# A new order of all steps, with the identity compared on VectorE, its reversal copied from it and fewer index iotas

## The chip, the cores and the metric

The kernel runs on one NeuronCore of a Trainium2 chip. Its engines work side by side, each through its own instructions in order: TensorE (PE in the profile, with its weight loads as PEld), VectorE (DVE), ScalarE (ACT), GpSimd (POOL) and SyncE (SP), which here only issues DMAs. An engine waits for another one by semaphores. The metric is the device time of one execution in microseconds (us).

## The reference

Two layers in a row, in float32. First an attention with a feature map instead of a softmax, for 8 batches and 8 heads of 576 positions by 64:

```python
def phi(x):
    proj = np.einsum('bhsd,df->bhsf', x, w_phi)          # 64 -> 128 features
    proj = proj - np.max(np.abs(proj), axis=-1, keepdims=True)
    return np.concatenate([np.exp(proj), np.exp(-proj)], axis=-1)
q_p, k_p = phi(q), phi(k)
kv  = np.einsum('bhsf,bhsd->bhfd', k_p, v);   z = np.sum(k_p, axis=2)
num = np.einsum('bhsf,bhfd->bhsd', q_p, kv);  den = np.einsum('bhsf,bhf->bhs', q_p, z)
x = num / (den + 1e-6)                                   # heads side by side: (8, 576, 512)
```

Then a gated convolution over the sequence, done with Fourier transforms of length 576:

```python
x1, x2, x3 = np.split(x @ w_proj, 3, axis=-1)            # 512 -> 3 * 512
H = np.fft.rfft(filter_fft, n=S, axis=0)
x2_conv = np.fft.irfft(np.fft.rfft(x2, n=S, axis=1) * H, n=S, axis=1)
out = (x1 * x2_conv * x3) @ w_out
```

## The kernel before

The eight batches are called images here. For each image the kernel does the same chain of steps, and the steps of several images are interleaved. Nothing is scheduled at run time or by a planner inside the kernel: one string, `PLAN`, lists all steps in order, and `run` goes through it word by word and calls the method of that name. Each engine therefore executes its instructions in the order in which the words stand. A word reads `name,arguments@bank`: `ex,k,p,1,1@6` is the exponential, k side, positive sign, image 1, block 1, from PSUM bank 6; `ACT`, `DVE` or `POOL` among the arguments says which engine does the step.

PSUM has eight banks, and the plan says which a step uses. A step that writes a bank waits until the one before it there has been read, and readers of one bank on different engines follow each other in plan order.

**The start.** Nothing of the transforms comes from memory: cosine and sine tables are made on the chip. `gen_part` and `gen_rows` write indices with iotas on POOL (lines 344 to 361; the tiles `part`, `fr`, `nr`). `gen_cols` makes some forty column constants on DVE (lines 379 to 423). `gen_whole` rounds index times constant to a whole number on ACT (line 435), `gen_angles` subtracts it on DVE (line 452), and `gen_sin` takes the sine on ACT (line 467) into the tables `D`, `Dt` and `inv`. `gen_ident` and `gen_back` make an identity and a reversal matrix on POOL, each by an iota and a compare with a constant (lines 305 to 316). The identity serves PE's transposes (`pt`, `ptx`, `trm`), the reversal a product `D1m` that mirrors `D`, which `D1e` copies out with signs (line 333). `gen_neg` stores negated copies of two tables (line 996). `filt_load`, `filt_fold`, `H`, `H_ev` and `H_cp` transform the filter.

**One image.** `load` fetches q, k and v through POOL's DMA queue (line 586) with a cast to bfloat16. `trh` transposes q and k by DMA on SP's queue (line 598), for image 0 `pt` and `pte` do it on PE and an evacuating engine (lines 608, 288 and 290; 288 is an ACT copy, 290 a DVE copy). `Pk` and `Qn` are the projections, `maxk` and `maxq` the absolute maxima on DVE (line 703), `mhi`, `mlo`, `trm` and `trme` bring q's maxima into rows, `Pq` projects q again with the maxima subtracted on PE. `ex`, `exkt` and `exqt` are the exponentials on ACT (lines 689 to 697), `em` those of the maxima, `vs` scales v with them (line 750). `KV` sums keys by values on PE (line 765), `KVe` copies it out, `NE` and `NEt` make numerator and denominator (lines 779, 788), `rc`, `xn`, `rct` and `xnt` divide (lines 793 to 815). The sequence of 576 is cut as 9 times 64; the names that end in `t` handle the ninth part. `trx` and `trxt` transpose x by DMA on SP (lines 822, 827), for image 0 `ptx` and `ptxt` do it on PE (lines 832, 841).

`f1` and `f2` are two levels of folds, sums and differences (lines 852, 858; tiles `SD` and `xf`), `F` is the forward transform on PE (lines 864, 868), `Fe` and `Fet` copy it out, `X2` applies the second third of the weights in the transformed domain (line 886), `Y1` multiplies by the filter (line 896), `m3` adds pairs (line 900), `I` is the inverse transform (line 973), with `Ie`, `Ip` and `Im` as its evacuation and half sums (lines 977, 980). `X1` and `X3` are the other two projections (line 908; `X1a` and `X1b` are half of one each), `X1e` copies one out, `tm` multiplies by the other (line 961). `ym` multiplies both branches (line 1021), `O` is the last product (line 1032), `Oe` copies it out, `st` and `sh` store halves of it (line 1041): `st` on SP, `sh` on ACT's or SP's queue as the word says. The last image uses `J` and `yj` (lines 1011, 1015) instead of `I`, `Ip`, `Im` and `ym`.

**What orders POOL against DVE.** The method `port` adds a dependency: after certain steps on DVE (those in the tuple `PORT` with `DVE` in their word, `gen_angles` and `yt`) the next listed POOL step waits for the DVE instruction. So a POOL step of that kind can wait for work on DVE whose data it doesn't use.

## Time and profile before

| what | us |
|---|---|
| median of 3 runs | 304.31 |
| lowest and highest run | 304.29 and 306.02 |
| the profiled execution | 304.55 |
| its span, first to last instruction | 302.8 |

The profile is of one execution, so instruction times and waits come from a run that lies 0.24 us above the median; its span leaves out 1.75 us around the first and the last instruction. The engine table of the page gives each engine's busy time and its share of the span. The stretches give the same by stage, with the granted clock of TensorE and the share of the DMA engines. The chain of work that ended last goes back from the last instruction through what released each step. In a timeline row the numbers are start, duration, engine, line, operation and tiles, with the idle time ahead of it and what ended that in brackets. A row of a group has the count, then the busy time in us and the mean of one in ns.

### The profile page before, as it was taken

How to read it: one execution, taken by the hardware profiler on the slowest of the kernel's cores; microseconds unless marked ns; L12 is line 12 of the kernel's file. 1: busy time of each engine (PE TensorE's matmuls, PEld its weight loads, DVE VectorE, ACT ScalarE, POOL GpSimd, SP SyncE). 2: the span in 40 equal slices, each digit the busy share in tenths (PEclk: the TensorE clock that was granted, in tenths of full speed). 3: DMA queues.
4: the chain of work that ended last, by engine and by line, in shares of the span. 5: the costliest groups of instructions: out<-in, count | busy, mean ns of one | idle time of the engine just before them, and what ended most of it. 6: DMA issues, size and time to landing. Idle time of an engine off the chain costs nothing.

```text
span 302.8 us, 10174 instructions
## 1 busy us (share of the span) xinstructions
PE 269.7 (89%) x4253; PEld 198.2 (65%) x4289; DVE 258.9 (86%) x449; ACT 227.8 (75%) x407; POOL 219.7 (73%) x190
## 2 busy tenths in 40 slices
...
GB/s 135 214 203 133 187 142 154 205 117 132 146 191 157 125 106 181 164 170 135 184 214 130 97 115 166 127 189 83 131 40 59 110 69 2 36 98 87 2 157 192
DMA packets 71902, 39.98 MB, mean 132 GB/s; under 512 B 52208, under 2 KB 66672, under 8 KB 71856
## 3 DMA queue, kind: packets, MB, share of 16 engines
...
## 4 chain that ended last, share of the span: by engine, by line
PE 67%; DVE 13%; ACT 8%; issue 5%; POOL 4%; DMA 1%; SPq 0%; DVEq 0%; ACTq 0%
PE ps L908 17%; PE ps L886 9%; PE ps L1032 9%; PE ps L973 5%; PE ps L765 5%; PE ps L779 3%; DVE mq L703 3%; DVE mk L703 2%; PE ps L864 2%; PE ps L868 2%; PE ps L627 2%; PE ps L917 2%; PE ps L661 2%; PE ps L1011 2%; PE ps L667 1%
## 5 line engine op out<-in xcount | busy, mean ns | idle before, releaser
L908 PE MATMUL ps<-xT,wproj 128*128 128x256 bf16 x512 | 64.8, 273 | 0.2
L908 PEld LDWEIGHTS <-wproj 128*128 128x128 bf16 x512 | 47.7, 98 | 9.4 <-issue 0.4
L703 DVE TENSOR_REDUCE mk<-ps 128x8 f32<-128x1024 f32 (+1 forms) x40 | 43.8, 1109 | 4.5 <-PE ps L627 2.2
L703 DVE TENSOR_REDUCE mq<-ps 128x8 f32<-128x1024 f32 (+1 forms) x40 | 44.1, 1110 | 2.9 <-PE ps L642 1.5
L852 POOL TENSOR_TENSOR SD<-xn 128x512 bf16<-128x512 bf16 x29 | 33.1, 1153 | 15.6 <-ACT xn L805 4.0
L750 POOL TENSOR_TENSOR vm<-vn,vm 128x1152 bf16<-128x1152 bf16 x15 | 32.3, 2153 | 9.2 <-ACT Eqp L689 4.1
L750 POOL TENSOR_TENSOR vp<-vn,vp 128x1152 bf16<-128x1152 bf16 x15 | 32.3, 2153 | 5.7 <-ACT vp L744 5.6
L689 ACT ACTIVATE Eqp<-ps 128x1024 bf16<-128x1024 f32 x32 | 32.7, 1025 | 3.8 <-PE ps L667 3.1
L1021 POOL TENSOR_TENSOR yT<-cv,x1s 128x576 bf16<-128x576 f32 x23 | 29.2, 1280 | 8.6 <-DVE yT L1021 4.1
L689 ACT ACTIVATE Ekm<-ps 128x1024 bf16<-128x1024 f32 x32 | 32.7, 1038 | 3.2 <-PE ps L627 2.4
L689 ACT ACTIVATE Eqm<-ps 128x1024 bf16<-128x1024 f32 x32 | 32.8, 1024 | 2.9 <-PE ps L667 2.9
L1032 PE MATMUL ps<-wout,yT 128*128 128x512 bf16 x133 | 33.7, 379 | 0.8 <-issue 0.2
L858 POOL TENSOR_TENSOR xf<-SD 128x512 bf16<-128x512 bf16 x29 | 33.0, 1153 | 1.5 <-PE ps L627 0.7
L689 ACT ACTIVATE Ekp<-ps 128x1024 bf16<-128x1024 f32 x32 | 32.9, 1046 | 1.6 <-DVE mk L703 1.6
L900 POOL TENSOR_TENSOR T<-T,T 128x1024 bf16<-128x1024 bf16 x12 | 25.4, 2122 | 9.7 <-DVE T L896 6.7
L886 PE MATMUL ps<-wproj,XF 128*128 128x512 bf16 x111 | 30.5, 380 | 1.0 <-issue 0.2
L288 ACT CAST x1s<-ps 128x512 bf16<-128x512 f32 (+1 forms) x27 | 15.1, 562 | 19.4 <-PE ps L908 14.4
L980 DVE TENSOR_TENSOR cv<-es,ps 128x288 f32<-128x288 f32 x56 | 22.4, 447 | 2.7 <-ACT es L977 2.0
L973 PE MATMUL ps<-inv,T 128*128 128x288 bf16 x168 | 24.3, 286 | 0.2
L961 DVE TENSOR_TENSOR x1s<-ps,x1s 128x512 bf16<-128x512 f32 x32 | 21.6, 682 | 3.1 <-ACT x1s L288 1.6
L1032 PEld LDWEIGHTS <-yT 128*128 128x128 bf16 x144 | 13.3, 98 | 14.1 <-DVE yT L1015 0.5
L779 PE MATMUL ps<-KVs,Eqp 128*128 128x65 bf16 x256 | 19.5, 192 | 1.6 <-DVE x1s L965 0.9
...
## 6 DMA issues: line engine op xcount, KB each, us to landing
...
```

Source lines behind the costliest of these rows:

```text
L689: self.nc.scalar.activation(e, p, AF.Exp, bias=0.0, scale=1.0 if g == "p" else -1.0)
L703: self.nc.vector.tensor_reduce(out=out, in_=src, axis=AX.X, op=ALU.max, apply_absolute_value=True)
L750: self.eng(eng).tensor_tensor(out=t[:, :, :, 0:64], in0=self.at("vn", b)[:, 2 * X:2 * X + 2], in1=t[:, :, :, 64:65].to_broadcast([128, 2, ...
L779: self.mm(self.pb(u, 65 * a, 65 * a + 65), E, KVs[:, u, v, s, :], start=(s == 0), stop=(s == 1))
L852: self.eng(eng).tensor_tensor(out=o[:, :, 2 * i:2 * i + 2, :], in0=x[:, :, 0:2, :], in1=x[:, :, 2:4, :], op=ALU.subtract if i else ALU.add)
L858: self.eng(eng).tensor_tensor(out=o[:, :, 2 * i:2 * i + 2, :], in0=x[:, :, 0:4:2, :], in1=x[:, :, 1:4:2, :], op=ALU.subtract if i else ALU ...
L886: self.mm(self.pb(0), l, w[:, kt, 512:1024], start=(kt == 0), stop=(kt == 3))
L900: self.eng(eng).tensor_tensor(out=Y, in0=Y, in1=self.at(f"T{2 * e + 1}", b), op=ALU.add)
L908: self.mm(o[:, d], w[:, kt, f0 + 128 * m:f0 + 128 * m + 128], y[:, 1, ::-1, ::-1] if d else y[:, 0], start=(kt == 0 and not d), stop=(kt = ...
L973: self.mm(self.pb(e, 0, 288), l, inv[:, 2 * e + i if i < 2 else 4 + e, :], start=(i == 0), stop=(i == 2))
L1021: self.eng(eng).tensor_tensor(out=self.at("yT", b)[:, m, 0:SEQ], in0=self.at("cv", 4 * b + m).rearrange("p x h t -> p (x h t)"), in1=self. ...
L1032: self.mm(self.pb(0), y[:, kt, 128 * c:128 * c + 128], w[:, kt, :], start=(kt == 0), stop=(kt == 3))
```

## The change

Five things, all in the diff below.

- The identity's compare moves from POOL to DVE (`gen_ident,DVE`); its iota is a step of its own, `gen_idx`. `gen_ident` joins `PORT`, so the POOL step that follows it in the listed set waits for it.
- The reversal matrix is no longer made from a second iota and compare; `gen_back,ACT` copies the identity with its columns in reverse.
- The row indices come from five iotas instead of nine; the larger ones write both halves of a tile at once.
- `xnt`, the division of the ninth part, takes an engine; on ScalarE it is four multiplications. The new plan names DVE for all sixteen.
- All steps stand in a new order with other banks, and many change engine: `D1e` goes to ACT and `gen_whole,3` to DVE; of the folds `f1` and `f2`, six go from DVE to POOL and three the other way; of `m3`, two go to POOL and four to DVE; of `ym`, four go to POOL and one to DVE; evacuations change between ACT and DVE in both directions. `gen_neg` moves from the middle of image 0 to the sines. The stores of image 6 and the last image are split anew between ACT's and SP's queues.

The steps are the same in number and work on TensorE. Of the plan, the diff is cut to the start, a stretch of image 3 and the end.

```diff
 PORT = ("f1", "f2", "m3", "vs", "ym", "mlo", "filt_fold", "gen_ends", "gen_five",
-        "gen_whole", "H_cp")
+        "gen_whole", "gen_ident", "H_cp")
...
-w_load,phi gen_part gen_cols,0 loadh,q,0,0 filt_loadt loadh,q,0,1 filt_load,3 gen_rows,0 w_phi
-gen_cols,1 filt_load,2 gen_rows,1 gen_whole,ACT,2 gen_ident filt_load,0 gen_back gen_whole,ACT,3
-gen_one gen_whole,ACT,0 loadh,k,0,1 gen_angles,3 filt_load,1 load,q,1 gen_whole,ACT,4 pt,q,0,0,0@0
-gen_angles,0 pt,q,0,0,1@1 loadh,k,0,0 gen_angles,2 pte,ACT,q,0,0,0@0 w_load,proj,2 gen_angles,4
-pte,ACT,q,0,0,1@1 load,v,0 gen_sin,0 Qn,0,0@0 filt_fold,DVE,2 gen_sin,4 D1m@2 maxq,0,0@0
-filt_fold,POOL,0 pt,q,0,1,0@4 pt,q,0,1,1@5 zeros pt,k,0,1,0@0 pte,DVE,q,0,1,0@4 gen_sin,2
-pte,DVE,q,0,1,1@5 pt,k,0,1,1@1 D1e,DVE@2 filt_fold,POOL,1 Qn,0,3@4 pte,DVE,k,0,1,1@1 Qn,0,1@6
-pte,DVE,k,0,1,0@0 gen_sin,3 maxq,0,1@6 Pk,0,3@0 H,0@2 trh,q,1,1 Pk,0,2@6 H_ev,DVE,0@2 ex,k,p,0,3@0
...
-f1,DVE,0,1,0 ptx,0,3@3 mhi,1 rct,0@4 Pk,1,0@0 ex,k,m,1,1@6 f1,POOL,0,1,1 ptxe,DVE,0,1@2 xnt,0,1@4
-xnt,0,0@4 ptxe,ACT,0,3@3 maxk,1,1@6 load,v,1 ptxt,0@4 X1a,0,1@5 ex,k,p,1,0@0 w_load,proj,1 Pkt,1@2
...
-m3,DVE,2,1 KVe,ACT,3,1@4 Pkt,4@0 NE,3,1@2 ex,q,m,3,3@6 m3,DVE,2,0 X2,2,4@4 trh,q,5,0 rc,3,1@2
-maxkt,4@0 ex,q,p,3,3@6 X3,2,2@5 xn,DVE,3,1@2 exkt,p,4@0 trh,k,5,0 Y1,2,4@4 NE,3,3@6 exkt,m,4@0
-NE,3,2@2 f1,DVE,3,0,0 mhi,4 rc,3,3@6 NEt,3@0 mlo,POOL,4 xn,DVE,3,3@6 trh,k,5,1 f1,POOL,3,0,1 O,1,4@4
...
-Oe,ACT,6,2@7 O,7,2@6 yt,ACT,7 st,6,2 O,7,0@7 Oe,ACT,7,2@6 O,7,4@5 sh,SP,7,2,0 sh,ACT,7,2,1
-Oe,DVE,7,0@7 O,7,3@6 Oe,DVE,7,4@5 sh,SP,7,0,0 sh,ACT,7,0,1 O,7,1@7 Oe,DVE,7,3@6 sh,SP,7,4,0
-sh,ACT,7,4,1 Oe,DVE,7,1@7 sh,SP,7,3,0 sh,ACT,7,3,1 sh,SP,7,1,0 sh,ACT,7,1,1
+w_load,phi gen_part gen_idx gen_cols,0 loadh,q,0,0 filt_loadt loadh,q,0,1 zeros filt_load,2
+gen_ident,DVE gen_one gen_rows,0 gen_cols,1 filt_load,3 gen_rows,1 gen_whole,ACT,0 loadh,k,0,1
+gen_whole,ACT,2 filt_load,1 load,q,1 w_phi gen_angles,0 gen_whole,ACT,4 loadh,k,0,0 gen_angles,2
+filt_load,0 load,v,0 gen_sin,0 gen_whole,DVE,3 pt,q,0,0,0@0 w_load,proj,2 gen_back,ACT pt,q,0,0,1@1
+gen_angles,4 pte,ACT,q,0,0,0@0 pte,ACT,q,0,0,1@1 gen_sin,2 gen_angles,3 Qn,0,0@0 filt_fold,DVE,2
+pt,q,0,1,0@2 maxq,0,0@0 filt_fold,POOL,0 gen_sin,4 D1m@4 pt,q,0,1,1@3 pte,DVE,q,0,1,0@2 pt,k,0,1,0@0
+pte,DVE,q,0,1,1@3 pt,k,0,1,1@2 gen_neg pte,DVE,k,0,1,0@0 Qn,0,3@6 gen_sin,3 pte,DVE,k,0,1,1@2
+Pk,0,3@2 D1e,ACT@4 Qn,0,1@0 maxq,0,1@0 H,0@4 trh,q,1,1 H_ev,DVE,0@4 Pk,0,2@0 ex,k,p,0,3@2 maxq,0,3@6
...
+load,v,1 X1a,0,2@7 ex,k,m,1,0@4 X1b,0,2@7 maxkt,1@0 w_load,proj,1 X1a,0,3@2 X1e,ACT,0,1@6 maxk,1,0@4
+X3a,0,1@3 f2,POOL,0,1,0 exkt,m,1@0 ptxt,0@6 X1b,0,3@2 exkt,p,1@0 X1e,DVE,0,2@7 ptxte,ACT,0@6
...
+rc,3,0@4 xn,DVE,3,0@4 X2,2,1@6 ex,q,m,3,2@2 maxk,4,0@0 m3,POOL,2,1 KV,3,1@4 trxt,2 mhi,4
+X1e,ACT,2,2@7 Y1,2,1@6 Pkt,4@0 trx,3,0 Pq,3,3@2 exkt,m,4@0 X3,2,2@7 KVe,DVE,3,1@4 m3,POOL,2,0
...
+ex,q,p,3,3@2 st,0,2 NE,3,2@0 Y1,2,4@6 f1,POOL,3,0,1 NEt,3@4 rc,3,2@0 trh,k,5,0 NE,3,3@2 xn,DVE,3,2@0
+O,1,4@6 f1,POOL,3,0,0 rc,3,3@2 xn,DVE,3,3@2 X1t,2@0 rct,3@4 Oe,ACT,1,4@6 f2,POOL,3,0,0 trx,3,3
...
+Oe,DVE,7,3@2 sh,ACT,7,1,0 O,7,4@4 Oe,DVE,7,2@1 sh,SP,7,3,1 sh,ACT,7,3,0 sh,ACT,7,2,0 Oe,DVE,7,4@4
+sh,SP,7,2,1 sh,ACT,7,4,1 sh,ACT,7,4,0
...
-    def gen_ident(self):
-        g, s = self.nc.gpsimd, self.scr
-        kw = dict(allow_small_or_imprecise_dtypes=True)
-        idx = s.tile([128, 128], FP32, name="idx")
-        g.iota(idx, pattern=[[1, 128]], base=0, channel_multiplier=-1, **kw)
-        self.idx = idx
-        g.tensor_scalar(out=self.at("ident"), in0=idx, scalar1=0.0, scalar2=None,
-                        op0=ALU.is_equal)
-
-    def gen_back(self):
-        g, s = self.nc.gpsimd, self.scr
-        idx = s.tile([128, 128], FP32, name="idy")
-        self.back = s.tile([128, 128], BF16, name="back")
-        g.iota(idx, pattern=[[1, 128]], base=0, channel_multiplier=1,
-               allow_small_or_imprecise_dtypes=True)
-        g.tensor_scalar(out=self.back, in0=idx, scalar1=127.0, scalar2=None, op0=ALU.is_equal)
+    def gen_idx(self):
+        self.idx = self.scr.tile([128, 128], FP32, name="idx")
+        self.nc.gpsimd.iota(self.idx, pattern=[[1, 128]], base=0, channel_multiplier=-1,
+                            allow_small_or_imprecise_dtypes=True)
+
+    def gen_ident(self, eng):
+        self.eng(eng).tensor_scalar(out=self.at("ident"), in0=self.idx, scalar1=0.0, scalar2=None,
+                                    op0=ALU.is_equal)
+
+    def gen_back(self, eng):
+        self.back = self.scr.tile([128, 128], BF16, name="back")
+        self.copy(eng, self.back, self.at("ident")[:, ::-1])
...
-            g.iota(self.nr[:, 0:128], pattern=[[1, 4], [9, 32]], base=1, **kw)
-            g.iota(self.nr[:, 128:256], pattern=[[1, 4], [9, 32]], base=6, **kw)
+            g.iota(self.nr[:, 0:256], pattern=[[5, 2], [1, 4], [9, 32]], base=1, **kw)
...
-        for odd in range(2):
-            g.iota(self.fr[:, odd, 0], pattern=[[2, 144]], base=odd, **kw)
-            g.iota(self.fr[:, odd, 1, 0:16], pattern=[[2, 16]], base=256 + odd, **kw)
-            g.iota(self.fr[:, odd, 1, 16:144], pattern=[[2, 128]], base=odd, **kw)
+        g.iota(self.fr[:, :, 0], pattern=[[1, 2], [2, 144]], base=0, **kw)
+        g.iota(self.fr[:, :, 1, 0:16], pattern=[[1, 2], [2, 16]], base=256, **kw)
+        g.iota(self.fr[:, :, 1, 16:144], pattern=[[1, 2], [2, 128]], base=0, **kw)
...
+        for X in range(2):
+            for u in range(2):
+                self.nc.scalar.mul(o[:, X, u, :], n[r, X, u, w, 0:64], rt[r, 2 * X + u, w, :])
...
-        elif f in PORT and "POOL" in args or f in ("gen_ident", "gen_back", "gen_part", "gen_rows"):
+        elif f in PORT and "POOL" in args or f in ("gen_idx", "gen_part", "gen_rows"):
```

309 lines of the change are left out of this document (157 added, 152 removed).

## The prediction

> **What bounds the kernel now.** I read the page first, then busy time by stretches, then the chain that ended last.
>
> ```profile
> span 302.8 us, 10174 instructions
> ...
> PE 269.7 (89%) x4253; PEld 198.2 (65%) x4289; DVE 258.9 (86%) x449; ACT 227.8 (75%) x407; POOL 219.7 (73%) x190
> ...
> PE 67%; DVE 13%; ACT 8%; issue 5%; POOL 4%; DMA 1%; SPq 0%; DVEq 0%; ACTq 0%
> ```
>
> PE is busy 89% of the span and holds 67% of the chain. But an average hides the stages, so here are three stretches (PE, PEld, DVE, ACT, POOL busy, then the granted clock):
>
> ```profile
> 10.00:20.00 10.00, 6.68 (x74) 4.87 (x76) 8.55 (x19) 9.95 (x17) 6.18 (x3) 1.00 1.20 210
> ...
> 200.00:240.00 40.00, 39.54 (x606) 29.42 (x607) 34.72 (x58) 32.90 (x56) 34.08 (x26) 1.00 0.46 88
> ...
> 285.00:302.80 17.80, 12.19 (x77) 7.25 (x75) 8.80 (x13) 1.50 (x4) 0.00 (x0) 0.92 0.60 148
> ```
>
> Three stages, three limits. At the start PE is idle a third of the time and ACT is full (9.95 of 10 us). In the body PE has 39.54 of 40 us, so no reordering can gain more than PE's few gaps: the matmuls stay the same. At the end 5.6 us are without PE: the last evacuation and the landing of the last stores.
>
> The chain through the start, and the rows that show what opened it:
>
> ```profile
> 2.99 0.28 POOL L358 IOTA fr<- 128x144 f32 x1
> ...
> 3.58 0.97 DVE L583 CAST wphi<-phi 128x128 bf16<-128x128 f32 x1 [1.13 <-DMA phi<-in_w_phi_dram]
> ...
> 5.73 1.15 ACT L435 ACTIVATE whole<-nr,cols 128x288 int16<-128x288 f32 x2 [0.89 <-DVE cols L417]
> ```
>
> ```profile
> 5.73 3.64 ACT whole L435 x7
> 9.37 1.05 ACT qT L288 x2
> ...
> 10.45 1.28 ACT L467
> ...
> 11.74 0.87 ACT D L467 x2
> 12.61 1.89 ACT inv L467 x4
> 14.50 1.86 ACT Dt L467 x4
> ...
> 18.54 1.02 ACT Ekp L689
> ```
>
> DVE waits 1.13 us for the phi weights and casts them in 0.97 us before it can finish the column constants; ACT waits 0.89 us for those; then seven roundings, two evacuations, a table load and the sines run without a gap until the first exponential at 18.54 us. What moves 18.54 moves all that follows, until PE fills up at about 45 us.
>
> **The change, part by part.** All sums are against the profiled run itself, 304.55 us (its span of 302.8 and 1.75 around it); that run is 0.24 us above the median of 304.31.
>
> *The start (0.0 us, between -0.5 and +0.9).* Prices of what moves:
>
> ```profile
> L307 POOL TENSOR_SCALAR ident<-idx 128x128 bf16<-128x128 f32 x1 | 0.6, 556 | 0.1
> ...
> L996 ACT ACTIVATE inv<-inv 128x576 bf16<-128x576 bf16 x1 | 0.7, 685 | 0.0
> ...
> L288 ACT CAST XFt<-ps 128x128 bf16<-128x128 f32 x20 | 5.3, 277 | 0.3 <-PE ps L868 0.3
> ...
> L290 DVE COPY xTt<-ps 128x256 bf16<-128x256 bf16 x1 | 0.3, 281 | 0.0
> ```
>
> POOL loses both compares (0.56 us for this one, the other alike) and five small iotas, so its loads after the first two leave 1 to 2 us sooner; transfers already fill the DMA engines there (share 1.20), so I count nothing for it. The phi cast now stands behind the column constants, so ACT's run opens when the row indices exist. POOL's first such iota stood at 2.99 us; with the idx iota ahead of it, and twice as long itself, I put its end at 3.7. Again seven roundings open the run (tables 0, 2 and 4; table 3 goes to DVE), so the run starts 5.73 - 3.7 = 2.0 us sooner. But ACT takes on three things ahead of its first exponential: the reversal copy (an ACT copy of 128 columns takes 0.28), the negation (0.69, formerly behind the exponentials of the first image) and the four parts of D1e (0.28 each, 1.1 in all). That is 2.07 us. 2.0 gained, 2.07 spent: the first exponential stays at 18.5. If the added operations overlap their neighbours it is 0.5 better. The upper end is the new wait: a port dependency makes POOL's row iotas wait for the identity compare on DVE, itself behind the first column constants and two memsets. Behind them on POOL stand the second row indices, five loads and the filter fold; ACT's first rounding and PE's k transposes wait for those. No row shows this compare on DVE. Below is half the 256-column copy's time (0.14), above the phi cast's 0.97; I take 0.2, since it stands beside DMA issues, not iotas. At 0.97 the row indices are 0.4 late, and the phi cast stretched again adds 0.5 ahead of the angles: +0.9.
>
> The 0.97 has a rule beside it: the Trainium skill, SBUF — State Buffer, section "Who interferes with whom", says that a VectorE copy, cast or tensor_scalar in a two-port mode and a GpSimd instruction hold the shared port in turn, the later one fully blocked. The cast ended when POOL's iotas did, which agrees. By it the compare would wait out a load issue on POOL and the start cost the upper end.
>
> *The first image (-1.3 us, between -1.4 and 0).* A fold and an evacuation on DVE, and the PE waits that I use, with what ended them:
>
> ```profile
> 43.45 0.41 DVE L852 TENSOR_TENSOR SD<-xn 128x512 bf16<-128x512 bf16 x1
> ...
> 43.90 0.37 DVE L290 COPY xT<-ps 128x512 bf16<-128x512 bf16 x1
> ```
>
> ```profile
> 45.20 0.28 PE L841 MATMUL ps<-ident,xnt 128*128 128x128 bf16 x2 [1.04 <-DVE xnt L815]
> ...
> 75.95 0.38 PE L627 MATMUL ps<-wphi,kT 64*128 64x128 bf16 x7 [0.37 <-DVE cv L980]
> ...
> 154.05 0.43 PE L765 MATMUL ps<-vp,Ekp 64*128 64x65 bf16 x15 [1.60 <-issue]
> ...
> 184.86 0.19 PE L779 MATMUL ps<-KVs,Eqp 128*128 128x65 bf16 x1 [0.39 <-ACT KVs L288]
> ...
> 186.89 0.43 PE L765 MATMUL ps<-vp,Ekp 64*128 64x65 bf16 x16 [0.55 <-DVE r L793]
> ...
> 190.90 0.20 PE L779 MATMUL ps<-KVs,Eqp 128*128 128x65 bf16 x1 [0.86 <-DVE x1s L965]
> ```
>
> The tail transpose `ptxt,0`, which held PE 1.04 us, moves behind six half projections, which need only the evacuated xT. Next late is `ptxe,0,1`, the row at 43.90: ahead of it on DVE a fold goes and another evacuation comes (0.41 and 0.37), so it still ends at 44.3, and the projections start there and not behind 45.20: -0.9. Later, one m3 of image 0 goes from POOL to DVE, out of a POOL queue of two m3, four folds and a ym whose end releases cv; PE's 0.37 at 75.95 goes: -0.4. Upper end: the waits only change their names.
>
> *The body (0, between -3.4 and +4.2).* Engine moves cancel: three folds net to POOL, two m3 net to DVE, three ym net to POOL, evacuations to and fro; PE covers them all, and with that cover gone they cost what the second rival counts. Of the waits above, 1.80 us (the last three) and the unexplained 1.60 could go; new ones can come at any of some 1400 moved steps. I take no difference. The new tail division on ScalarE is nowhere called (all sixteen `xnt` say DVE): 0.
>
> *The end (+0.5 us, between 0 and +0.9).*
>
> ```profile
> L1041 SPq DMA_DIRECT2D out_dram<-o x67: 466/588/1187, 112.7 to 298.0; - x67
> ...
> L1041 ACTq DMA_DIRECT2D out_dram<-o x5: 497/498/569, 294.5 to 298.0; - x5
> ```
>
> ```profile
> 263.06 3.81 SPq L822 DMA_TRANSPOSE xT<-xn x3
> ```
>
> Both queues' last issue stood at 298.0: one half of the last block on each. Now the last block's halves are both on ACT's queue, one behind the other, 0.50 us. Nothing follows that hides it. On SP, image 7's four transposes now run in the order 3, 0, 2, 1, the first behind a division that ScalarE does; at 1.27 us an issue (the row at 263.06) the last one is issued 3.8 us behind the first and has then to land, where `X3,7,1` comes after about 6 us of products (seven of 0.86 or less). I count nothing, and 0.4 in the upper end. Elsewhere SP's transposes and stores trade places with whole products between them and their users.
>
> Sum: 0 - 1.3 + 0 + 0.5 = -0.8, so 303.75 against the profiled run, 303.5 against the median.
>
> **The rivals.**
>
> *Waits go (faster).* The new order also removes the three late waits and the 1.60: -0.8 - 1.8 - 1.6 = -4.2, 300.1. For it: each is one step's place. Against: 1.60 is put down to nothing that an order could mend.
>
> *POOL becomes the bound (slower).* In image 3 the old order gave both m3 and one fold to DVE; POOL then stood idle. The new one gives POOL all of it.
>
> ```profile
> 122.52 2.15 POOL L750 TENSOR_TENSOR vm<-vn,vm 128x1152 bf16<-128x1152 bf16 x1
> ...
> 130.25 0.25 POOL L727 TENSOR_TENSOR mh<-mq,mh 128x36 bf16<-128x36 f32 x1 [5.58 <-DVE r L793]
> ```
>
> ```profile
> L852 POOL TENSOR_TENSOR SD<-xn 128x512 bf16<-128x512 bf16 x29 | 33.1, 1153 | 15.6 <-ACT xn L805 4.0 <-DVE xn L800 3.6 <-DVE SD L852 3.0
> ...
> L900 POOL TENSOR_TENSOR T<-T,T 128x1024 bf16<-128x1024 bf16 x12 | 25.4, 2122 | 9.7 <-DVE T L896 6.7 <-DVE r L793 3.0
> ```
>
> ```profile
> 125.11 0.43 PE L765 MATMUL ps<-vp,Ekp 64*128 64x65 bf16 x16
> ...
> 138.15 0.41 PE L864 MATMUL ps<-Dt,xnt 128*128 128x288 bf16 x2
> ...
> 169.22 0.91 PE L973 MATMUL ps<-inv,T 128*128 128x288 bf16 x6
> 169.96 1.03 PE L1032 MATMUL ps<-wout,yT 128*128 128x512 bf16 x4
> 170.82 0.90 PE L973 MATMUL ps<-inv,T 128*128 128x288 bf16 x6
> ```
>
> From the end of vs at 124.67, two m3 (2.12) and six folds (1.15) take 11.1 us: 135.8. PE went from `KV,3,1` at 125.11 to `F,3,0` at 138.15 and now does so without one inverse (0.74, start to start) and one output product (0.86): 136.55. 0.75 us of slack. It decides once POOL is over 0.75 late, for instance waiting for xn. One such miss of 0.7 at each of images 1 to 6 is +4.2: -0.8 + 4.2, 307.7. For it: the slack was 5.58 us and is now 0.75. Against: in the other images loads are nearly as before.
>
> *Table loads (slower).* ACT now puts copies and a negation between sines, which no row shows: the 10.45 load stands behind the copies. If those need another table, the reversal, the next sine, the negation and the sine after it each load one: 4 x 1.28 = +5.1 on the full engine, 308.6. The Trainium skill, ScalarE: Activation LUTs, "Table sets: the hidden batching unit", says cheap functions such as copy stand in every set; by that it costs nothing. It is why I leave this a small chance.
>
> **How the numbers follow.** Forecast 0.60 (its own range 301.5 to 306.0), waits go 0.15, POOL 0.18, tables 0.07. 1% of 304.31, about what a measurement of this kernel can tell from no change, sets 301.3 and 307.4. So faster 0.15, same 0.60, slower 0.25. The range takes in most of the first two rivals and the bounds of the start and end: 300.3 to 308.0.
>
> **What would show it.** The first exponential at 18.5 (within 0.6), with three table loads; no wait of a microsecond ahead of `ptxt,0`; about 5.6 + 0.5 us without PE at the end; POOL without its 5.58 us gap and `F,3,0` not waiting for xf. Wrong it is if PE's waits between 60 and 285 us sum to over 3 us more or less than now, or if the first X1 is over 1.5 us off 44.3.

## The result and the profile after

| | before | after |
|---|---|---|
| median, us (18 runs each, side by side) | 305.44 | 307.87 |
| lowest to highest | 303.14 to 308.29 | 305.51 to 311.91 |
| the profiled execution | 304.55 | 306.96 |
| its span | 302.8 | 305.2 |

The changed kernel takes 1.0071 times as long [1.0046, 1.0096]: 2.2 us slower, where 0.8 us faster was forecast. On the median of 304.31 that is 306.5. The two profiled executions lie 2.41 us apart, so the traces show what the medians show. The profiled executions of two experiments, e10 and e18, were disturbed, and of these only the ratio and the start are used.

The page after, same lines as shown of before:

```profile
span 305.2 us, 10167 instructions
...
PE 272.3 (89%) x4257; PEld 199.4 (65%) x4289; DVE 254.0 (83%) x435; ACT 228.6 (75%) x410; POOL 221.8 (73%) x189
...
PE 60%; DVE 11%; DMA 8%; POOL 7%; issue 5%; ACT 5%; SPq 1%; DVEq 0%; POOLq 0%
```

PE has the same work and the same share. In the chain DMA now has 8% (1% before) and POOL 7% (4%). The stretches, with the same columns as before:

```profile
10.00:20.00 10.00, 7.26 (x66) 4.72 (x68) 6.08 (x10) 9.97 (x21) 2.91 (x2) 1.00 1.20 217
...
200.00:240.00 40.00, 39.68 (x617) 29.89 (x619) 34.71 (x57) 33.85 (x59) 29.61 (x23) 1.00 0.72 121
...
285.00:305.20 20.20, 13.71 (x87) 8.38 (x87) 9.95 (x16) 2.35 (x4) 0.00 (x0) 0.93 0.43 111
```

ACT is still full at the start, PE still full in the body; the last stretch begins at the same 285 and lasts 2.4 us longer. To see where the time goes, I read the start of the same matmul groups in both timelines (TensorE's work ahead of each is the same within 0.1 us):

| PE reaches, us | before | after | difference |
|---|---|---|---|
| first projection of image 0 | 45.32 | 44.65 | -0.67 |
| `KV,1,1` | 66.89 | 67.13 | +0.24 |
| `KV,3,0` | 118.70 | 120.52 | +1.82 |
| `KV,5,0` | 182.86 | 184.66 | +1.80 |
| `KV,6,0` | 212.01 | 212.02 | +0.01 |
| `KV,7,1` | 257.11 | 257.11 | 0.00 |
| end of the last matmul | 297.25 | 298.82 | +1.57 |
| end of the span | 302.8 | 305.2 | +2.4 |

The body loses 1.8 us and wins it back, and at 257.11 both kernels stand level. In these two executions the whole loss arises behind that point. That they meet to the hundredth is chance: from `KV,1,1` to `KV,7,1` PE takes 190.22 us before and 189.98 after, but 190.3 to 191.4 in the profiles of e1, e2, e3 and e5, experiments below that leave this stretch as it is. The loss and the gain within it recur in all of them. The waits of PE after (columns as before: start, busy time, instruction, and in brackets the idle time ahead and what ended it):

```profile
44.65 1.05 PE L910 MATMUL ps<-xT,wproj 128*128 128x256 bf16 x8
...
54.27 0.40 PE L623 MATMUL ps<-wphi,kT 64*128 64x128 bf16 x8 [0.42 <-DVE XF L292]
...
72.85 1.63 PE L975 MATMUL ps<-inv,T 128*128 128x288 bf16 x12 [0.46 <-DVE xn L796]
...
89.64 0.43 PE L761 MATMUL ps<-vp,Ekp 64*128 64x65 bf16 x16 [0.94 <-POOL vp L746]
...
98.50 0.71 PE L910 MATMUL ps<-xT,wproj 128*128 128x256 bf16 x5 [0.61 <-issue]
...
155.45 0.42 PE L761 MATMUL ps<-vp,Ekp 64*128 64x65 bf16 x15 [1.26 <-issue]
...
161.64 0.19 PE L775 MATMUL ps<-KVs,Eqp 128*128 128x65 bf16 x1 [0.78 <-issue]
...
270.61 0.93 PE L910 MATMUL ps<-xT,wproj 128*128 128x256 bf16 x7 [1.41 <-DMA xT<-xn]
```

Between 60 and 285 us all waits of over 0.15 us, with those not shown, sum to 7.30 us, against 5.73 before. Three things stand out, and the experiments follow them: the wait for `xT` at 270.61 with a longer end behind it; waits of 0.4 to 1.6 us put down to "issue", in both kernels, around 155 and 160; and a first projection that is earlier without the first image being done earlier.

### The profile page after: what moved, and what is told of

It reads as the page before. It is cut to its first block, busy times and chain, and to the rows that moved or that the text cites. A ratio compares the mean times of both kernels' runs of the same rounds, so it can differ in the third digit from the quotient of the medians.

```text
span 305.2 us, 10167 instructions
## 1 busy us (share of the span) xinstructions
PE 272.3 (89%) x4257; PEld 199.4 (65%) x4289; DVE 254.0 (83%) x435; ACT 228.6 (75%) x410; POOL 221.8 (73%) x189
## 3 DMA queue, kind: packets, MB, share of 16 engines
q10 hardware_dynamic: 960, 1.57, 1.9%
## 4 chain that ended last, share of the span: by engine, by line
PE 60%; DVE 11%; DMA 8%; POOL 7%; issue 5%; ACT 5%; SPq 1%; DVEq 0%; POOLq 0%
PE ps L910 13%; PE ps L888 9%; PE ps L1034 9%; PE ps L761 5%; PE ps L975 4%; PE ps L775 4%; DVE mk L699 3%; DVE mq L699 3%; DMA vn<-in_v_dram 3%; DMA fl<-in_moe_filter_fft_dram 2%; PE ps L866 2%; PE ps L870 2%; POOL SD L854 2%; PE ps L623 2%; PE ps L657 2%
## 5 line engine op out<-in xcount | busy, mean ns | idle before, releaser
L910 PE MATMUL ps<-xT,wproj 128*128 128x256 bf16 x512 | 65.8, 273 | 2.2 <-DMA xT<-xn 1.4
L854 POOL TENSOR_TENSOR SD<-xn 128x512 bf16<-128x512 bf16 x31 | 35.3, 1152 | 10.3 <-DVE xn L796 4.7
L1023 POOL TENSOR_TENSOR yT<-cv,x1s 128x576 bf16<-128x576 f32 x26 | 33.0, 1279 | 10.7 <-DVE cv L982 7.9
L1034 PE MATMUL ps<-wout,yT 128*128 128x512 bf16 x135 | 34.7, 379 | 0.6
L860 POOL TENSOR_TENSOR xf<-SD 128x512 bf16<-128x512 bf16 x30 | 34.2, 1155 | 1.5 <-DVE xf L860 0.6
L902 POOL TENSOR_TENSOR T<-T,T 128x1024 bf16<-128x1024 bf16 x10 | 21.2, 2122 | 13.5 <-DVE T L898 12.2
L888 PE MATMUL ps<-wproj,XF 128*128 128x512 bf16 x111 | 29.4, 380 | 1.3 <-issue 0.5
L290 ACT CAST XF<-ps 128x512 bf16<-128x512 f32 x30 | 17.5, 592 | 8.8 <-PE ps L870 4.9
L1034 PEld LDWEIGHTS <-yT 128*128 128x128 bf16 x144 | 13.3, 98 | 14.0 <-DVE yT L1017 0.5
```

Of the source, the lines that this page charges most:

```text
L290: self.nc.scalar.copy(dst, src)
L854: self.eng(eng).tensor_tensor(out=o[:, :, 2 * i:2 * i + 2, :], in0=x[:, :, 0:2, :], in1=x[:, :, 2:4, :], op=ALU.subtract if i else ALU.add)
L860: self.eng(eng).tensor_tensor(out=o[:, :, 2 * i:2 * i + 2, :], in0=x[:, :, 0:4:2, :], in1=x[:, :, 1:4:2, :], op=ALU.subtract if i else ALU ...
L888: self.mm(self.pb(0), l, w[:, kt, 512:1024], start=(kt == 0), stop=(kt == 3))
L910: self.mm(o[:, d], w[:, kt, f0 + 128 * m:f0 + 128 * m + 128], y[:, 1, ::-1, ::-1] if d else y[:, 0], start=(kt == 0 and not d), stop=(kt = ...
L1023: self.eng(eng).tensor_tensor(out=self.at("yT", b)[:, m, 0:SEQ], in0=self.at("cv", 4 * b + m).rearrange("p x h t -> p (x h t)"), in1=self. ...
```

## The experiments

Each diff is cut to the words that move. Ratios are to the kernel before on the same chip, with the 95% interval.

### The end: transposes in the wrong order, and one buffer too few

All four transposes of image 7 stand on SP's queue in the order 3, 0, 2, 1, behind a division on ScalarE. The profile after, in rows of ScalarE and SP and the time to landing of these transposes:

```profile
260.52 1.75 ACT L801 ACTIVATE xn<-ps,r 128x64 bf16<-128x64 f32 x8 [0.24 <-POOL xf L860]
...
262.30 5.12 SPq L824 DMA_TRANSPOSE xT<-xn  x4
...
DMA to landing us min/median/max: 2.4/2.4/4.4
```

The queue begins when the division ends, the fourth transpose is issued at 266.17, and it takes 4.4 us to land where the rest take 2.4. At 2.4 it would have been there at 268.6, ahead of the 269.2 at which PE was ready for it (270.61 less the wait of 1.41). The trace shows what is late: a transpose reports in sixteen parts, and of this one's fifteen are there by 268.78 and the last at 270.56. Between them, at 268.55, a piece of PE's own program starts through the DMA engines (these pieces are told of below). Its row in the DMA view from 268.5 to 268.6 us:

```profile
q8 instruction: 1, 0.02, 57.4%
```

Little else moves there: the DMA engines are busy for 0.24 of the time from 268 to 270 us.

**e1** issues the two transposes whose data is ready early ahead of that division:

```diff
-xn,DVE,7,1@6 Y1,6,2@5 ... trx,7,3 ... trx,7,0 ... trx,7,2 ... trx,7,1
+xn,DVE,7,1@6 trx,7,0 trx,7,1 Y1,6,2@5 ... trx,7,3 ... trx,7,2
```

> The changed kernel with one edit: on SP's queue the transposes trx,7,0 and trx,7,1 (their divisions are done some 10 us earlier) are issued ahead of trx,7,3 instead of behind it. Theory (the queue's head: all four wait behind one division that ScalarE does in eight parts): the last transpose lands before X3,7,1 needs it, PE's wait of 1.41 us ahead of X3,7,1 goes to under 0.2, the last matmul ends 1.2 to 1.6 us sooner, the time falls by 1.4 us (306.5 to 305.1 for a kernel before of 304.3). Rival (the transposes land late because they land two at a time, 4.4 us where 2.4 is usual, or another wait takes the place): the wait stays above 0.8 or moves to the next products, and the time falls by less than 0.5.

Measured: 1.0049 [1.0016, 1.0081]. PE has no wait ahead of `X3,7,1`, all landings take 2.4 to 2.5 us, and from `KV,7,1` to the last matmul PE takes 40.14 us: the kernel before took 40.14, the changed one 41.71. So the 1.57 us at the last matmul are this wait, and the order of issue decides whether it is paid. That the piece is what held the last part up is likely and not tested by itself. In eighteen profiles (all but e10 and e18) 106 of 1134 such transposes have their last part over 1.5 us behind the others; in 101 of these a piece had started 1.9 to 2.5 us ahead of that landing, against 110 of the other 1028. And e4 below, which has the changed kernel's order of issue but its pieces at other matmuls, waits only 0.42 there.

The remaining 0.83 us lie behind the last matmul. **e2** puts one half of the last block back on SP's queue:

```diff
-sh,SP,7,2,1 sh,ACT,7,4,1 sh,ACT,7,4,0
+sh,SP,7,2,1 sh,ACT,7,4,1 sh,SP,7,4,0
```

> The changed kernel with one edit: of the last output block's two halves one goes to SP's queue again and one to ScalarE's. Theory (the second issue of 0.5 us on one queue sets the end): from the last matmul to the end 5.5 to 5.9 us instead of 6.4, time 0.5 to 0.8 lower. Rival (the landing of the last stores sets the end, whichever queue): under 0.2.

Measured: 1.0085 [1.0049, 1.0121]; from the last matmul to the end 6.76 us, not less than the 6.38 after. By itself this doesn't clear the two issues, since the copies here still end 1.27 us behind the last matmul, as after. The next run does: it keeps both halves on ACT's queue, and its end is as long as before's to about 0.1 us.

**e5** exchanges output blocks 2 and 3 of the last image, products, copies and stores alike:

```diff
-O,7,3@2 ... O,7,2@1 ... Oe,DVE,7,3@2 ... Oe,DVE,7,2@1 ... sh,SP,7,3,1 sh,ACT,7,3,0 sh,ACT,7,2,0
+O,7,2@2 ... O,7,3@1 ... Oe,DVE,7,2@2 ... Oe,DVE,7,3@1 ... sh,SP,7,2,1 sh,ACT,7,2,0 sh,ACT,7,3,0
```

> The changed kernel with output blocks 2 and 3 of image 7 exchanged in the last steps (products, evacuations, stores); the work is the same. Theory (the six output buffers: block 3 of image 7 takes the buffer of block 2 of image 6, whose store has just been issued, so VectorE's last three evacuations wait for that landing from 297.1 to 298.2 and end 1.27 us behind the last matmul, where they ended 0.72 behind it before the change): the first of the three starts at once, the last evacuation ends 0.7 to 0.8 us behind the last matmul, from the last matmul to the end 5.7 to 5.9 us instead of 6.4, time 0.5 lower. Rival (the stores' landing or the queue sets the end): the evacuations come sooner and the end stays within 0.2 of 6.3.

The last matmuls and last evacuations of DVE, first before, then after, then e5:

```profile
291.74 5.51 PE L1032 MATMUL ps<-wout,yT 128*128 128x512 bf16 x23
...
296.47 1.50 DVE L290 COPY o<-ps 128x512 f32<-128x512 f32 x2 [0.23 <-PE ps L1032]
```

```profile
293.31 5.51 PE L1034 MATMUL ps<-wout,yT 128*128 128x512 bf16 x23
...
298.20 1.89 DVE L292 COPY o<-ps 128x512 f32<-128x512 f32 x3 [1.11 <-PE ps L1034]
```

```profile
294.09 5.51 PE L1034 MATMUL ps<-wout,yT 128*128 128x512 bf16 x24
...
298.82 1.50 DVE L292 COPY o<-ps 128x512 f32<-128x512 f32 x2 [0.23 <-PE ps L1034]
```

Before, the last copy ends 0.72 us behind the last matmul (297.25 to 297.97); after, 1.27 (298.82 to 300.09), because DVE stood 1.11 us and three copies then follow each other. e5 is back at 0.72 (299.60 to 300.32), and from the last matmul to the end at 5.60 (before 5.55). The bracket names PE, but the product had been done: there are six output buffers, used in turn, and in the new order the first of the three copies gets the buffer of an image-6 block whose store is among the last issued. The copy waited for that store. The time of e5 alone, 1.0073 [1.0036, 1.011], doesn't show it: other waits of its profiled run, in the body, are 1.2 us longer.

**e10** has both repairs, the diffs of e1 and e5 together:

> The changed kernel with both edits at the end together: image 7's transposes 0 and 1 ahead of the one that waits for ScalarE, and its output blocks 2 and 3 exchanged. Theory (the two are the last 41 us' loss and add up): no wait ahead of X3,7,1, from KV,7,1's first matmul to the last matmul 39.6 us instead of 41.1, from there to the end 5.6 instead of 6.4, the time 2.0 to 2.3 below the changed kernel and so within 0.3% of before. Rival (they hide one another, or the rest of the order is as much at fault): less than 1 us, still 0.4% or more above before.

Measured: 1.0013 [0.9978, 1.0047]. Of the 0.71% that the change cost, 0.58 went with these few moved words, 1.8 us of 2.2, a difference known to about 0.4%. So the end is the loss as far as the times tell: what is left, 0.13%, lies within its interval. Three more kernels below have both repairs, e12, e14 and e16; in their profiles PE takes 40.14 us from `KV,7,1` to the last matmul, and from there to the end it is 5.6 to 5.8. (e15, which has them too, takes 40.14 and 6.2.)

### The start: an earlier exponential that nothing uses

DVE, POOL and ACT after, in time order within each fence:

```profile
2.46 0.16 DVE L309 TENSOR_SCALAR ident<-idx 128x128 bf16<-128x128 f32 x1
```

```profile
3.00 0.42 POOL L354 IOTA fr<- 128x288 f32 x1
...
14.69 2.35 POOL L515 TENSOR_TENSOR fe<-fl 128x1024 bf16<-128x1024 f32 x1 [6.56 <-DVE kT L292]
```

```profile
3.45 2.04 ACT L431 ACTIVATE whole<-fr,cols 128x288 int16<-128x288 f32 x4 [1.43 <-POOL fr L354]
...
14.17 0.67 ACT L998 ACTIVATE inv<-inv 128x576 bf16<-128x576 bf16 x1
...
15.59 0.79 ACT L329 ACTIVATE D<-ps 128x144 bf16<-128x144 f32 x4
16.40 1.28 ACT L685 ACT_TABLE_LOAD   x1
17.70 1.03 ACT L685 ACTIVATE Ekp<-ps 128x1024 bf16<-128x1024 f32 x1
```

The compare took 0.16 us (0.2 was taken), and POOL's row iota stands at 3.00, where it was at 2.99: the new wait costs nothing. ACT's run opens at 3.45 and its first exponential stands at 17.70, 0.84 sooner than before. The compare (2.46 to 2.62) lies inside a load issue of POOL (2.26 to 3.01). The Trainium skill, SBUF — State Buffer, section "Who interferes with whom", has the later of the two fully blocked if the compare runs in a two-port mode. No block shows here, and no run tells in which mode it ran. The phi cast, 0.97 us beside POOL's iotas before, now takes 0.44.

But the filter fold on POOL, at 13.58 before, now stands at 14.69, and PE waits for it:

```profile
17.09 0.58 PE L533 MATMUL ps<-fe,D 128*128 128x512 bf16 x1 [1.21 <-POOL fe L515]
```

The bracket at 14.69 names a DVE copy, yet the filter itself had only just come. These are its last two pieces in the DMA view (from 6 to 15 us), before and after, with the size and the median us to landing:

```profile
fl<-in_moe_filter_fft_dram SPq DMA_DIRECT2D x2, 128.0 KB, 6.4
```

```profile
fl<-in_moe_filter_fft_dram SPq DMA_DIRECT2D x2, 128.0 KB, 7.5
```

**e8** asks whether the constants or the order matter: the order of before, with the new way to make identity, reversal and indices.

```diff
-gen_rows,1 gen_whole,ACT,2 gen_ident filt_load,0 gen_back
+gen_rows,1 gen_whole,ACT,2 gen_idx gen_ident,DVE filt_load,0 gen_back,DVE
```

> The order of before, with the changed ways of making the constants alone (compare on VectorE, reversal copied from it, there on VectorE, the fewer iotas). My prediction's reasoning (ACT's run opens when VectorE's column constants are done, whatever POOL does): first exponential at 18.5 within 0.4, time within 0.5 of before. Theory of the new start's cost (POOL's loads leave 1.5 to 2 us sooner and share the DMA engines with the filter rows): the fold begins 0.5 to 1 us later than 13.6, the first filter product waits, and the time is 0.5 to 1 us more than before. If it is over 0.7 us faster than before, the new constants are the gain and the new order loses it.

Measured: 0.9994 [0.9952, 1.0036]; first exponential at 18.08, fold at 14.90, first projection at 45.32, where before has 45.32. The new constants cost or gain less than 0.5%, and in the profile the first projection doesn't move: what the change did came from the order, as far as that tells.

**e3** moves two loads that left before the filter's last pieces, `load,v,0` and `w_load,proj,2`, behind the fold; **e6** moves `load,q,1` there:

```diff
-filt_load,0 load,v,0 gen_sin,0 ... w_load,proj,2 ... filt_fold,POOL,0
+filt_load,0 gen_sin,0 ... filt_fold,POOL,0 load,v,0 w_load,proj,2
```

> The changed kernel with two POOL issues moved: the load of v of image 0 and the third projection load go behind POOL's first filter fold. Theory (the loads, which now leave 2 us sooner, share the DMA engines with the filter rows, so the fold begins at 14.7 instead of 13.6 and PE waits 1.2 for it at 17.1): the fold begins at 13.7 or sooner, the wait at 17.1 falls under 0.3, HTe is evacuated at about 17.6 and the reductions behind it move up, the first projection starts 0.5 to 0.9 us sooner. Rival (DVE's reductions set the start from 18 us on whatever the filter does): the wait goes but the first projection stays within 0.3 of 44.65 and the time within 0.4. A late v may cost instead: then vs of image 0 waits for its load.

```diff
-filt_load,1 load,q,1 w_phi ... filt_fold,POOL,0
+filt_load,1 w_phi ... filt_fold,POOL,0 load,q,1
```

> The changed kernel with one POOL issue moved: the load of q of image 1 goes from between the two halves of k to behind POOL's first filter fold. Theory (what leaves first shares the DMA engines with the filter rows and the second half of k; v and the projection, behind them, did not matter): the filter rows land and the fold begins about 1 us sooner (13.7 instead of 14.7), PE's wait of about 1 us ahead of the first filter product at 17.1 goes under 0.4, k's transposes no longer wait, the first exponential stays, the first projection starts 0.5 or more sooner than 44.65. Rival (bytes of k and the filter alone fill the time): fold at 14.4 or later, nothing moves by more than 0.3.

Measured: 1.0106 [1.0069, 1.0142] with the fold at 14.75, and 1.0093 [1.0049, 1.0137] with the fold at 15.18. Both theories fall: none of these three loads alone holds the filter back. The other loads that leave sooner, the halves of k at 4.37 and 5.83 us (6.17 and 7.69 before), were moved by no run. The fold starts at 13.3 to 14.0 in the profiles where the loads leave as before (before, e11, e17), and at 13.9 to 15.8 where they leave sooner. So that the loads hold the filter back is likely, and not shown.

**e18** (on e15, below) lets ScalarE's queue fetch half of the filter, beside the other half on SP's. In the plan `filt_load,1` and `filt_load,0` move up to right behind `filt_load,2`, and:

```diff
-            self.nc.sync.dma_start(out=self.fl[32 * i:32 * i + 32, ...
+            (self.nc.sync if a > 1 else self.nc.scalar).dma_start(out=self.fl[32 * i:32 * i + 32, ...
```

> The run with both edits at the end and both loads' places mended, with half of the filter rows issued on ScalarE's queue ahead of its table load instead of behind the other half on SP's. Theory (in the new order the first projection follows the first filter fold by 30.0 us within 0.4, in seventeen profiles between 13.9 and 15.8 for the fold, and nothing else of the start): the rows leave 2 us sooner and are ahead of k in the DMA engines, the fold begins at 12.5 to 13.6, the first projection at 42.8 to 43.7 (44.7 without), although the first exponential comes 0.6 later (18.3) behind the four issues; time 1 us below the run without this edit, 0.8 to 1.1% below before. Rival (the first exponentials and VectorE's reductions bind as soon as the fold is 1 us sooner, or the bytes of q and k fill the engines anyway): fold at 14 or later, or the first projection at 44.4 or later, and the time level with or above the run without it.

(The profiles it counts are fifteen, not seventeen.) Measured: 1.0000 [0.9965, 1.0036], where e15 has 0.9938. POOL, ACT and PE in e18:

```profile
12.48 2.36 POOL L515 TENSOR_TENSOR fe<-fl 128x1024 bf16<-128x1024 f32 x1 [4.43 <-DMA fl<-in_moe_filter_fft_dram]
```

```profile
19.11 1.02 ACT L685 ACTIVATE Ekp<-ps 128x1024 bf16<-128x1024 f32 x1
```

```profile
17.50 0.39 PE L533 MATMUL ps<-fe,D 128*128 128x512 bf16 x1 [1.32 <-ACT D L329]
```

The fold is 2.2 us earlier, and now the wait is for ACT, whose run the four issues and a later q (PE starts at 7.76, not 6.01) put back by 1.4. The start has two arms, ACT's run and the filter. In fifteen profiles of the new order the first projection follows the fold's start by 29.4 to 30.1 us (13.9 gives 43.38, 14.69 gives 44.65, 15.82 gives 45.67; e7 alone has 31.2, with a wait of 1.25 for a piece of PE's program in between) while the first exponential stays at 17.70 to 17.86; in the order of before it stays at 45.2 to 45.3 with the fold anywhere from 13.3 to 14.9 (e17 apart, where a wait for nothing, of the kind told of below, put it back). Which of the other transfers makes the fold vary by 2 us from one execution to the next stays open.

### The first image: waits that change their names

The 1.04 us ahead of `ptxt,0` are gone. **e11** moves this one word in the order of before:

```diff
-load,v,1 ptxt,0@4 X1a,0,1@5 ... X1a,0,2@6 load,k,2 ptxte,DVE,0@4
+load,v,1 X1a,0,1@5 ... X1a,0,2@6 load,k,2 ptxt,0@4 ptxte,DVE,0@4
```

> The kernel before with one step moved: the transposes ptxt,0 of the first image's tail go behind six half projections' worth of PE work, to just ahead of their evacuation. My prediction's step for this edit: PE's wait of 1.04 us ahead of them goes, the first projection starts 0.6 to 0.9 us sooner, and the body keeps it: time 0.6 to 0.9 (0.2 to 0.3%) below before. Rival (VectorE, 98% busy from 45 to 60 us, sets that stage): the wait goes, another of 0.4 or more comes ahead of Pk or F products by 60 us, KV,1,1 starts within 0.3 of where it did (66.9 us; 21.6 from the first projection before, then longer), time within 0.2 us.

Measured: 1.0022 [0.9987, 1.0056]. The wait stays and only stands elsewhere, in PE's row of e11:

```profile
45.20 0.60 PE L908 MATMUL ps<-xT,wproj 128*128 128x256 bf16 x4 [1.03 <-DVE xnt L815]
```

The first projection's bank is held by the division too, which reads banks 4 and 5 as one tile; in the new order the projection has bank 6, and the division reads 0 and 1. It was the new order's banks together with the place that removed the wait. What came instead, 0.42 at 54.27 and 0.46 at 72.85, **e7** tries to mend: `tm,0,1` moves behind the evacuation for which PE waits.

```diff
-F,0,2@4 tm,0,1@3 X1e,ACT,0,0@2 F,0,3@0 Fet,DVE,0,2@4 Fe,DVE,0,2@4
+F,0,2@4 X1e,ACT,0,0@2 F,0,3@0 Fet,DVE,0,2@4 Fe,DVE,0,2@4 tm,0,1@3
```

> The changed kernel with VectorE's product tm,0,1 moved behind the two evacuations of F,0,2 in the first image. Theory (PE's new wait of 0.42 us ahead of Pk,1,2 at 54.3 is for the bank that these evacuations free, and tm stands ahead of them): the wait goes under 0.1 and the second pair of KV of image 1 starts 0.3 to 0.4 us sooner after the first projection (19.06 us from 44.65 to X1 .. KV,1,1 now 67.13 - 44.65 = 22.5, then 22.1). Rival (VectorE is full there, and the next product that needs it waits instead): the wait goes and KV,1,1 keeps its 22.5 us behind the first projection within 0.15.

```profile
55.27 0.38 PE L630 MATMUL ps<-wphi,qT 64*128 64x128 bf16 x7 [1.11 <-DVE x1s L963]
```

Measured: 1.01 [1.0031, 1.0169]. The 0.42 is gone, 1.11 stands in its place with 0.50 and 0.31 behind it, and from the first projection to `KV,1,1` PE takes 23.59 us, where the changed kernel takes 22.48. The stretch from 45 to 60 after, columns as above:

```profile
45.00:60.00 15.00, 14.18 (x186) 10.01 (x184) 14.37 (x20) 14.24 (x26) 12.26 (x12) 1.00 0.99 161
```

DVE is busy 14.37 of 15 us: an exchange on a full engine only chooses who is late.

### The waits for nothing: PE's own program

The "issue" waits stand at the same place in the program whichever order it has. Counted from 0, the matmul behind each is number 351, 2271, 2399 in both kernels (351 with only 0.28 us before; before also 2783 and 2911, after also 1375): always 95 more than a multiple of 128. A queue of its own carries "instruction" packets; its row in the page, the same before and after, and that of the DMA view from 153.0 to 153.2 us after:

```profile
q8 instruction: 33, 0.54, 0.8%
```

```profile
q8 instruction: 1, 0.02, 30.0%
```

33 packets make 0.54 MB, 16 KB each; PE's 4289 weight loads and as many matmuls (the page has 4257, since some records are missing) are 33 times 256 and some more, so a packet is 128 pairs. After, packets start at 96.0, 153.1 and 159.1, and the three waits end at 98.50, 155.45 and 161.64; before, 151.8 and 157.6 go with 154.05 and 159.97: 2.3 to 2.6 us each. If that is PE waiting for its own next instructions, then matmuls that are added must move the waits.

**e4** adds 32 small matmuls early in image 0:

```diff
-pt,q,0,0,1@1 gen_angles,4
+pt,q,0,0,1@1 pad@7 gen_angles,4
+    def pad(self):
+        ident = self.at("ident")
+        for i in range(32):
+            self.mm(self.pb(0, 0, 32), ident, ident[:, 0:32], True, True)
```

> The changed kernel with 32 more small matmuls of the identity early in the start, where PE waits for qT; their result is never read. Theory (PE's unexplained waits are its own program arriving late, in pieces of 128 matmuls with their 128 weight loads, always at the 95th matmul of a piece): the long waits that no semaphore explains come 32 matmuls earlier in PE's order: the one of 1.26 us leaves the first matmul of KV,4,1 and stands some 32 matmuls earlier, in the products ahead of it, that of 0.61 in X3,1,1 moves into or ahead of KV,2,1, that of 0.61 in KV,0,1 moves from the 13th of its second Ekm run to about the middle of KV,0,1. Rival (something at these steps, such as a bank or a semaphore that the profile doesn't show): they stay at the same matmuls. The time is not what this run is for; within 2 us of the changed kernel.

PE's first such wait after, and then the waits of e4:

```profile
38.34 0.22 PE L761 MATMUL ps<-vm,Ekm 64*128 64x65 bf16 x3 [0.61 <-issue]
```

```profile
37.33 0.19 PE L767 MATMUL ps<-vm,Fkm 64*128 64x65 bf16 x1 [0.94 <-issue]
...
91.49 0.19 PE L767 MATMUL ps<-vm,Fkm 64*128 64x65 bf16 x1 [1.56 <-issue]
...
100.43 0.59 PE L767 MATMUL ps<-vm,Ekm 64*128 64x65 bf16 x15 [3.61 <-issue]
...
197.72 0.51 PE L925 MATMUL ps<-xTt,wproj 128*128 128x64 bf16 x12 [1.82 <-issue]
```

Of the four waits after, three (351, 1375 and 2399) stand 32 matmuls earlier in the work, at the same number counting the added ones. At 2271 none is left, and new ones stand at 1247, 1759, 1887 and 2911, again 95 more than a multiple of 128. Pieces fall into new hot places: 3.61 at 100.43. These and three shorter ones (0.70, 0.81 and 0.89) make 10.3 us, where the changed kernel has four with 3.3. The run took 314.87 us, some 7 more than the changed kernel, for 32 matmuls of 32 columns; it is a single run, and some of its transposes land late as well. The Trainium skill, Runtime: NRT & Kernel Launch, section "Instruction fetch mechanics", states that an engine's program comes in blocks of 16 KiB, 256 instructions, over a DMA queue of its own, which the packets here agree with; it calls the cost "mostly hidden", and that the traces don't bear out.

A piece is late where 128 matmuls pass quickly (one `KV` is 72 of them in 1.3 us) while loads and transposes fill the DMA engines. The trace after shows when a piece sets out: as PE passes matmul 95 of the piece before. Where the DMA engines have little to do the packet starts at once (PE passes at 259.62 and 268.56, and the packet starts within 0.1 us), and where they are full (share 1.16 to 1.28) it starts 2.6 to 5.1 us later (2.58 behind 150.52, 3.48 behind 92.56, 5.11 behind 153.97). No run tried this by itself. Seven kernels move the loads around these places.

**e9** moves the loads of image 6, issued at 147.2 and 148.0, 8 us up; **e13** moves `load,k,4`, issued at 86.6, up behind `load,k,3`; **e12** puts both diffs on e10, **e14** the second alone on e10.

```diff
-I,2,2@2 load,k,6 Y1,3,1@7 X2,3,2@4 em,m,4,1 load,q,6
+f2,POOL,3,1,1 load,k,6 load,q,6
```

> The changed kernel with the loads of k and q of image 6 issued some 7 us earlier on POOL (behind the last fold of image 3, at about 140 instead of 147 us). Theory (PE's program arrives in pieces of 128 matmuls, and a piece's transfer stands in the DMA engines behind whatever bytes were issued before it): the wait inside KV,4,1, 1.3 to 2.6 us in the six kernels of this order so far, falls under 0.4, the one inside NE,4 (0.5 to 1.1 where it stood) does not grow by more than 0.5, and the time falls by 1 to 2 us. Rival (the piece takes its 3 to 6 us whatever else moves): both waits stay, the time within 0.5 of the changed kernel.

```diff
-load,k,3 f2,DVE,1,1,1 ... Fe,ACT,1,2@2 load,k,4
+load,k,3 load,k,4 f2,DVE,1,1,1 ... Fe,ACT,1,2@2
```

> The changed kernel with one POOL issue moved: the load of k of image 4 goes out at about 80 us, as in the old order, instead of 86.6. Theory (it is this place of the load that costs the middle: its bytes stand ahead of k's transposes of image 3 and of a piece of PE's program): the wait in X3,1,1 at 98.5 (0.5 to 1.2 us) goes under 0.3, the one ahead of KV,2,0 (0.3 to 1.2) under 0.3, from KV,1,1 to KV,3,0 52.3 us instead of 53.4 to 53.6, and the time is 1.0 to 1.5 us below the changed kernel. Rival (in the run that had it together with other edits these waits went for another reason, such as the start): both stay, the time within 0.4 of the changed kernel.

> The changed kernel with both edits at the end, with the loads of k and q of image 6 some 7 us earlier, and with the load of k of image 4 at 80 us as in the old order instead of 86.6, where it goes out right ahead of k's transposes of image 3. Theory (what the new order loses is the end and the program's late pieces): the unexplained wait in X3,1,1 at 98.5 (0.5 to 1.2 us in all kernels of this order, none in the old one) goes under 0.3, that in KV,4,1 under 0.4, and with the end the time is 3 to 4.5 us below the changed kernel, 0.5 to 1% below before. Rival (the freed waits are taken up by VectorE or POOL): within 0.3% of before.

> The changed kernel with both edits at the end and the load of k of image 4 at its old place. Theory (end 2 us, load over 1 us, and both in different stages): 3.0 to 3.5 us below the changed kernel, 0.2 to 0.5% below before. Rival (the DMA engines' next collision takes the load's gain): as with the end alone, 0.1% above before.

Measured: e9 1.0087 [1.0044, 1.013], e13 1.0061 [1.0024, 1.0098], e12 1.0002 [0.9969, 1.0034], e14 1.0022 [0.9988, 1.0056]. PE in e9, ACT in e12 and PE in e13:

```profile
151.67 0.61 PE L630 MATMUL ps<-wphi,qT 64*128 64x128 bf16 x8 [3.21 <-ACT o L290]
```

```profile
149.91 0.59 ACT L290 COPY o<-ps 128x512 f32<-128x512 f32 x1 [3.86 <-DMA out_dram<-o]
```

```profile
92.68 0.19 PE L775 MATMUL ps<-KVs,Eqm 128*128 128x65 bf16 x1 [1.11 <-issue]
```

In e9 the waits at 155 and 161 are gone, but the stores of image 1 are late, then the output buffers, then ACT, then PE: 3.21 us. e12 shows the middle of that chain. In e13 the wait at `KV,2,0` goes and the next piece is late instead, 1.11 at matmul 1247; from `KV,1,1` to `KV,3,0` PE takes 53.57 us, after 53.39. In both kernels what the move took away came back with another transfer.

**e15** (on e14) and **e16** (the same with `load,k,4` back in its place) move the loads of image 6 the other way, 13 us later, to 160 us, and their transposes behind `trx,4,2`:

```diff
-I,2,2@2 load,k,6 Y1,3,1@7 X2,3,2@4 em,m,4,1 load,q,6 ... trh,k,6,1 ... trh,k,6,0 ... trh,q,6,0 ... trh,q,6,1
+load,v,5 load,q,6 load,k,6 rc,4,3@4 ... trx,4,2 trh,q,6,0 trh,q,6,1 trh,k,6,1 trh,k,6,0
```

> The same as the run with both edits at the end and the load of k of image 4 early, and k and q of image 6 loaded behind the load of v of image 5 (at about 162 us) instead of 147, with their transposes behind image 4's. Theory (the loads at 147 fill the DMA engines when the piece of PE's program for KV,4,1 is due; later there is slower work on PE and nothing of these loads is needed before 175): the wait in KV,4,1 (1.3 to 2.6) goes under 0.5 and that in NE,4 under 0.6, no stores wait as they did with the loads at 140, and the time is 1 to 2 us below the run without this move, 0.7 to 1.1% below before. Rival (the bytes collide with something else wherever they go): a new wait of 1 us or more between 160 and 200 us, the time within 0.5 of the run without it.

```diff
-load,k,3 load,k,4 f2,DVE,1,1,1 ... Fe,ACT,1,2@2
+load,k,3 f2,DVE,1,1,1 ... Fe,ACT,1,2@2 load,k,4
```

> The changed kernel with both edits at the end and the loads of image 6 late, the load of k of image 4 where the new order has it. Theory (the loads of image 6 are the gain, the load of k of image 4 only moves a wait from 98.5 to 92.7): the waits in KV,4,1 and NE,4 are gone, the one at 98.5 is there, the time within 0.4% of the run that had the load of image 4 early too, 0.3 to 0.9% below before. Rival (both loads count): 0.4% or more above it, level with before.

Measured: 0.9938 [0.9904, 0.9971] and 0.9941 [0.9902, 0.9981]. Both beat the changed kernel and the one before, e15 with a median of 303.63 us beside 305.80 of before. PE in e15:

```profile
174.87 0.81 PE L910 MATMUL ps<-xT,wproj 128*128 128x256 bf16 x6 [0.58 <-DMA xT<-xn]
...
192.14 0.29 PE L638 MATMUL ps<-wphi,kT 64*128 64x128 bf16 x4 [2.13 <-DVE T L898]
```

No wait stands at 155 or 161. A new one stands at matmul 2911 (a piece again, though the bracket names DVE). This profiled execution, 305.26, is 1.6 us above its median, so the profile shows which waits went and came, but not the whole gain; 0.6 of the 1.6 is the longer end, 6.2 us.

**e17** does the same in the order of before (with `load,q,7`, behind `mlo,POOL,5`, and q's transposes behind `trx,4,0`):

```diff
-maxq,5,3@2 load,q,6 ... X2,3,2@1 load,k,6 ... I,2,2@2 load,q,7
+mlo,POOL,5 load,q,6 load,k,6 load,q,7
```

> The kernel before with one thing moved: the loads of q and k of image 6 and q of image 7 from 145 us to behind POOL's mlo of image 5 (some 15 us later), and the transposes of q of image 6 behind image 4's last. Theory (late pieces of PE's program are put down to the place of the loads, not to the new order): the waits at 154.05 (1.0 to 1.6 in this order) and 160.0 (0.4 to 0.8) go under 0.4 each and the time falls by 1 to 2 us, 0.3 to 0.7% below before. Rival (in this order another transfer stands in the way, or q of image 6 comes too late for its products at about 175 us): a new wait takes it, within 0.2% of before or slower.

Measured: 1.0104 [1.0057, 1.0151], slower. The wait at 155 is 0.87 in place of 1.60 and that at 160 is gone, but 1.24 and 1.40 stand at 189.33 and 193.88 (before 0.55 and 0.86 at 186.89 and 190.90), and two of 0.4 at 176 and 179. How much of the loss is the edit's the trace doesn't tell: this execution is 2.8 us longer than before's, and 2.3 of that stand ahead of the first projection (47.64 for 45.32), far ahead of the loads that move, 1.6 of it in a longer wait for a piece of PE's program (1.93 for 0.28). From `KV,1,1` to `KV,7,1` PE takes 190.89 us, for 190.22 before. So the place of these loads is no remedy by itself: it gains nothing in this order.

## Why the prediction was wrong, point by point

**What bounds the kernel: right.** PE has 39.68 of 40 us in the body, and the end and the waits decide. **The start (0.0): right in its price, wrong in what follows.** The compare is 0.16, three table loads stand as before, and the first exponential is at 17.70, sooner than the 18.5 given and 0.2 beyond the 0.6 allowed: ACT's run opens at 3.45 (3.7 was taken), and D1e's four parts take 0.79 (1.1). The step that failed is "transfers already fill the DMA engines there, so I count nothing for it": the filter's last pieces land later (7.5 us, not 6.4), and the fold is 1.1 later. That it is the loads leaving sooner that do this is likely and not shown. "What moves 18.54 moves all that follows" failed with it: the filter is a second arm.

**The first image (-1.3): wrong.** The first projection stands at 44.65 (44.3 said, -0.67 got), but at `KV,1,1` the change is 0.24 behind. The true case was the upper end of that term, "the waits only change their names": 0.42 at 54.27 and 0.46 at 72.85 for the 1.04 and 0.37 that went. From the first projection to `KV,1,1` PE takes 0.91 us more than before (22.48 for 21.57): 0.42 is that wait, 0.28 are the two transposes of `ptxt`, which now stand in this stretch, and the rest are shorter waits. e11 shows that the place of `ptxt,0` alone does nothing.

**The body (0): right in sum, -0.24 us between `KV,1,1` and `KV,7,1`**, though it is +1.6 and then -1.8 on the way. Of the four waits that could go, those at 186.89 and 190.90 went (1.41 us); that at 184.86 stayed (0.39, now 0.46 at 186.66) and so did the 1.60 (now 1.26). "Put down to nothing that an order could mend" was half right: the pieces come at fixed matmuls, but e15 and e16 show that what is in the DMA engines at that time can be chosen.

**The end (+0.5): here the sum failed most.** It is +2.4. The step that failed is the last transpose of image 7, which "has then to land", and of which I wrote "I count nothing, and 0.4 in the upper end". It cost 1.41 in the wait and 1.57 at the last matmul, and e1 takes all of it away. The order of issue was read rightly, four issues of 1.27 us behind a division, and at the usual 2.4 us the landing would have come 0.6 us ahead of PE. It took 4.4, its last part 1.8 us behind the other fifteen, with a piece of PE's program passing between them; the sum left no room for a late landing. The other 0.83 was forecast as 0.50 for two issues on one queue: about the size, but by luck, since the mechanism was another. e5 keeps the two issues and is back at the end of before: the cost was an output buffer whose store had not landed.

In one sum: +0.24, -0.24, +1.57, +0.83 makes +2.4, where the prediction had 0, -1.3, 0, +0.5 for start, first image, body and end; the +0.24 is start and first image together. So two terms were missed, the first image by 1.5 and the end by 1.9.

**The rivals.** Waits go: 1.41 of its 3.4 us went, and as much came elsewhere. POOL: its 5.58 us gap in image 3 is gone as said, but between 98.50 and 155.45 PE has no wait over 0.2 us, so `F,3,0` doesn't wait and 0.75 us of slack was enough. Table loads: dead, with three loads; this agrees with the Trainium skill, ScalarE: Activation LUTs, "Table sets: the hidden batching unit". "Wrong it is if PE's waits sum to over 3 us more or less": they are 1.57 more, about the size of the one wait at 270.61 (1.41), while as much went and came among the others. So this bound on the body said nothing of the end.

**What stays open.** Why from `KV,1,1` to `KV,3,0` the new order takes 1.58 us more: the named waits account for 1.38 of it (2.67 us against 1.29), chiefly 0.94 at `KV,2,0` and 0.61 at 98.50, and e13 moved these without a gain. Which transfers hold the filter up, and whether a piece of PE's program is what made one transpose land in 4.4 us, rest on the times in the traces and on no run that moved that alone. Ratios here are good to about 0.35%, so differences of one microsecond between two experiments are carried by the traces, not by the times.
